# Left queries in 128-wide slices, W1 cast by DMA, and a scheduler for three of five engines

## The chip, the cores and the metric

The kernel runs on one core of a Trainium2 chip. It is timed on the device, in microseconds, from launch to end; lower is better. The engines are TensorE (PE in the profile; PEld its weight loads), VectorE (DVE), ScalarE (ACT), GpSimd (POOL) and SyncE (SP, which here only issues DMAs).

## What is computed

Attention with normalised queries and keys over 8 batches, 12 heads, 448 tokens and 64 elements a head; then a layer normalisation and a two-layer network over the 768 joined elements of each token, added to its input. Inputs and output are FP32.

```
q_n, k_n = rmsnorm(q, g_q), rmsnorm(k, g_k)          # x / sqrt(mean(x*x) + 1e-6) * g
scores = q_n @ k_n.T / 8
attn = exp(scores - max) / (sum + 1e-9)
x = attn @ v                                          # (8, 448, 768)
xn = (x - mean) / sqrt(var + 1e-6) * g_ln
out = x + relu(xn @ w_ch1) @ w_ch2                    # 768 -> 3072 -> 768
```

## The kernel before

**Attention.** Heads go in pairs; a batch has 6 pairs, the kernel 48. q, k and v are loaded by units of 4 heads (two pairs, 24 units), into a tile `t` of 14 groups of 64 elements per partition: 6 groups for each pair's 384 tokens, in three j slices of 128, and one group for its 64 left tokens, of which one head's stand in partitions 0 to 63 and the other's in 64 to 127. `prep_unit` squares q and k on ScalarE, sums on VectorE, takes 1/sqrt by `_rsqrt` (an exponential as first guess, three Newton steps of four operations), multiplies k by g_q*g_k (`gprod`) and by its root, splits it into a high and a low FP16 part side by side (`khl`), and writes q twice side by side (`qn`). v is cast on GpSimd.

`trans_k` and `trans_q` bring each pair's seven 128x128 tiles through TensorE into `ps`, and VectorE copies them to `kT` and `qT`. `scores` makes seven matmuls per pair of 128 keys by 448 queries, the last one (left keys of both heads) in pieces; ScalarE takes the exponential into `E`. `values` multiplies: for each of the seven key tiles, three matmuls with 128 queries as weights (`oA`, L202) and one with the 64 left queries as weights (`oB`, L204). `evac_o` divides by the row sums and writes into the token tiles `x` (three of 128 tokens) and `xl` (left tokens of two batches).

**MLP.** `ln` normalises a batch (three tiles of 128 tokens; a batch of odd number has the left tokens of two batches as a fourth), `ln_trans` transposes into `xnT`. `up` makes `psH` (24 groups of 6 matmuls, 384 or 512 wide) and ScalarE the relu into `hT`; `down` makes `psC` (24 matmuls of 384 for each half tile), VectorE adds x, SyncE stores.

**Weights.** W1 comes in 12 pieces through a staging tile by the SP queue, and GpSimd multiplies each by g_ln into FP16 (`load_w1`, L264). W2 is cast by a DMA from GpSimd's queue (`load_w2`, L268).

**Order.** `run` interleaves: attention is a generator, and after each piece of MLP b it is driven on to the pairs of batch b+1, so that they are through at 0.78 of the MLP's work. The MLP of batch 0 starts after pair 6's scores. The last MLP has no attention beside it. A list scheduler of the kernel's framework then sets the order on all five engines from this text and the dependencies. A second path, `_general`, which a flag chooses where row sums fall outside a range, does not run here.

Of the kernel before, what the change touches and what calls it, by code (L numbers as in the profile page):

```python
# [10 lines left out]
INT32 = mybir.dt.int32  # L11
# [6 lines left out]
LN2 = 0.6931471805599453  # L18
# [5 lines left out]
NU = 3  # L24
UH = H // NU
UG = UH * 3 + UH // 2
EXP_BIAS = -4.0
REC_LO, REC_HI = 1.0 / 3.0e7, 0.5


def _rsqrt(nc, eng, out, a, t0, t1, iters=3):
    eng.tensor_copy(out=t0, in_=a.bitcast(INT32))
    eng.tensor_scalar(out=t0, in0=t0, scalar1=2.0 ** -23, scalar2=-127.0,
                      op0=ALU.mult, op1=ALU.add)
    nc.scalar.activation(out, t0, AFT.Exp, scale=-0.5 * LN2)
    for _ in range(iters):
        eng.tensor_tensor(out=t1, in0=out, in1=out, op=ALU.mult)
        eng.tensor_tensor(out=t1, in0=t1, in1=a, op=ALU.mult)
        eng.tensor_scalar(out=t1, in0=t1, scalar1=-0.5, scalar2=1.5, op0=ALU.mult, op1=ALU.add)
        eng.tensor_tensor(out=out, in0=out, in1=t1, op=ALU.mult)  # L40
# [6 lines left out]
class _Fast:  # L47


    def __init__(self, ctx, tc, sh, q, k, v, w1, w2, out):  # L50
# [5 lines left out]
        self.p_t = pool("p_t", 1)  # L56
# [6 lines left out]
        self.p_st = pool("p_st", 2)  # L63
# [7 lines left out]
        self.v16 = [fix.tile([128, UH, 3, D + 1], FP16, name=f"v{i}", tag=f"v{i}") for i in range(3)]  # L71
        self.vl = [fix.tile([128, UH // 2, 2, D + 1], FP16, name=f"vl{i}", tag=f"vl{i}")
                   for i in range(3)]
        for t in self.kT:
            nc.vector.memset(t[:, 1], 0.0)
        for t in self.v16:
            nc.vector.memset(t[:, :, :, D], 1.0)
        for t in self.vl:
            nc.vector.memset(t, 0.0)
            nc.vector.memset(t[0:64, :, 0, D], 1.0)  # L80
            nc.vector.memset(t[64:128, :, 1, D], 1.0)
        self.rec = fix.tile([128, B * NPAIR, 3, 2], FP32, name="rec_all", tag="rec_all")
# [6 lines left out]
    def load_unit(self, u):  # L89
        nc = self.nc  # L90
        b, hs = u // NU, (u % NU) * UH
        t = self.p_in.tile([128, 3, UG, D], FP32, tag="qkv")
        for n, src in enumerate((self.q, self.k, self.v)):
            nc.sync.dma_start(
                t[:, n, 0:UH * 3].rearrange("p (h j) d -> p h (j d)", j=3),
                src[b, hs:hs + UH, 0:384].rearrange("h (p j) d -> p h (j d)", j=3))
            left = src[b, hs:hs + UH, 384:448].rearrange("(g e) p d -> e p g d", e=2)
            for e in range(2):
                nc.sync.dma_start(t[64 * e:64 * e + 64, n, UH * 3:UG], left[e])
        self.loads[u] = t  # L100

    def prep_unit(self, u):
        nc, sh = self.nc, self.sh
        t = self.loads.pop(u)
        ssq = self.p_n.tile([128, 2, UG], FP32, tag="ssq")
        for n in range(2):
            sq = self.p_t.tile([128, UG, D], FP32, tag="sq", name="sq")
            nc.scalar.activation(sq, t[:, n], AFT.Square)  # L108
            nc.vector.tensor_reduce(out=ssq[:, n], in_=sq, axis=AX.X, op=ALU.add)  # L109
        msq = self.p_n.tile([128, 2, UG], FP32, tag="msq")  # L110
        nc.vector.tensor_scalar(out=msq, in0=ssq, scalar1=1.0 / D, scalar2=1e-6,
                                op0=ALU.mult, op1=ALU.add)
        rr = self.p_n.tile([128, 2, UG], FP32, tag="rr")
        t0 = self.p_n.tile([128, 2, UG], FP32, tag="rt0")
        t1 = self.p_n.tile([128, 2, UG], FP32, tag="rt1")
        _rsqrt(nc, nc.vector, rr, msq, t0, t1)
        qn = self.p_n.tile([128, UG, 2, D], FP16, tag="qn")
        khl = self.p_n.tile([128, UG, 2, D], FP16, tag="khl")
        nc.vector.tensor_tensor(out=t[:, 1], in0=t[:, 1],
                                in1=sh.gprod.unsqueeze(1).broadcast_to([128, UG, D]), op=ALU.mult)  # L120
        nc.vector.tensor_tensor(out=t[:, 1], in0=t[:, 1],
                                in1=rr[:, 1].unsqueeze(2).broadcast_to([128, UG, D]), op=ALU.mult)
        nc.vector.tensor_copy(out=khl[:, :, 0], in_=t[:, 1])
        nc.vector.tensor_tensor(out=khl[:, :, 1], in0=t[:, 1], in1=khl[:, :, 0], op=ALU.subtract)  # L124
        nc.vector.tensor_tensor(out=qn[:, :, 0], in0=t[:, 0],  # L125
                                in1=rr[:, 0].unsqueeze(2).broadcast_to([128, UG, D]), op=ALU.mult)
        nc.vector.tensor_copy(out=qn[:, :, 1], in_=qn[:, :, 0])
        v16, vl = self.v16[u % 3], self.vl[u % 3]
        nc.gpsimd.tensor_copy(out=v16[:, :, :, 0:D],  # L129
                              in_=t[:, 2, 0:UH * 3].rearrange("p (h j) d -> p h j d", j=3))  # L130
        for e in range(2):
            nc.gpsimd.tensor_copy(out=vl[64 * e:64 * e + 64, :, e, 0:D],
                                  in_=t[64 * e:64 * e + 64, 2, UH * 3:UG])
        self.units[u] = (qn, khl, v16, vl)


    def trans_k(self, p):
        nc, sh = self.nc, self.sh
        qn, khl, v16, vl = self.units[p // 2]
        w = p % 2  # L140
        ps = self.ps_tr.tile([128, 1024], FP16, tag="tr")
        kT = self.kT[p % 2]
        gs = [UH * 3 + w] + [6 * w + i for i in range(6)]
        for i, g in enumerate(gs):
            nc.tensor.matmul(ps[:, ts(i, 128)], khl[:, g], sh.id16, is_transpose=True,  # L145
                             start=(i == 0), stop=(i == 6))
        flat = kT.rearrange("p g d -> p (g d)")
        nc.vector.tensor_copy(out=flat[:, 0:64], in_=ps[:, 0:64])  # L148
        nc.vector.tensor_copy(out=flat[:, 128:960], in_=ps[:, 64:896])  # L149

    def trans_q(self, p):
        nc, sh = self.nc, self.sh
        qn, khl, v16, vl = self.units[p // 2]
        w = p % 2
        ps = self.ps_tr.tile([128, 1024], FP16, tag="tr")
        qT = self.p_qT.tile([128, 896], FP16, tag="qT")
        gs = [6 * w, 6 * w + 1, 6 * w + 2, UH * 3 + w, 6 * w + 3, 6 * w + 4, 6 * w + 5]
# [3 lines left out]
        nc.vector.tensor_copy(out=qT, in_=ps[:, 0:896])  # L161
        self.prs[p] = dict(qT=qT, kT=self.kT[p % 2])

    def scores(self, p, i):
# [6 lines left out]
        ps = self.ps_s.tile([128, 512], FP32, tag="psS")  # L171
# [11 lines left out]
    def values(self, p, i):  # L183
        nc = self.nc
        c = self.prs[p]
        qn, khl, v16, vl = self.units[p // 2]
        w = p % 2
        E = c["E"]
        if i == 0:
            c["oA"] = self.ps_o.tile([128, 3, 130], FP32, tag="oA", name="oA")  # L190
            c["oB"] = self.ps_o.tile([64, 130], FP32, tag="oB", name="oB")
        oA, oB = c["oA"], c["oB"]
        if i < 6:
            h, j = divmod(i, 3)
            rhs = v16[:, 2 * w + h, j]
            cs = slice(65 * h, 65 * h + 65)
            m0, l0 = (0, 384) if h == 0 else (64, 0)
        else:
            rhs = vl[:, w].rearrange("p e d -> p (e d)")
            cs, m0, l0 = slice(0, 130), 0, 384  # L200
        for t in range(3):
            nc.tensor.matmul(oA[:, t, cs], E[:, i, m0 + 128 * t:m0 + 128 * t + 128], rhs,  # L202
                             start=(i == 0 and t == 0), stop=(i == 6 and t == 2))
        nc.tensor.matmul(oB[:, cs], E[:, i, l0:l0 + 64], rhs, start=(i == 0), stop=(i == 6))  # L204
# [3 lines left out]
    def evac_o(self, p):  # L208
        nc = self.nc
# [5 lines left out]
        rec, recl = self.rec[:, p], self.recl[:, p]  # L215
        nc.vector.reciprocal(rec, oA[:, :, :, D])
        nc.vector.reciprocal(recl, oB[:, :, D])
        nc.vector.tensor_tensor(  # L218
            out=x[:, :, 128 * hp:128 * hp + 128].rearrange("p t (e d) -> p t e d", e=2),
            in0=oA[:, :, :, 0:D], in1=rec.unsqueeze(3).broadcast_to([128, 3, 2, D]), op=ALU.mult)  # L220
# [3 lines left out]
            in0=oB[:, :, 0:D], in1=recl.unsqueeze(2).broadcast_to([64, 2, D]), op=ALU.mult)  # L224

    def attention(self):

        n = B * NPAIR
        self.load_unit(0)
        self.load_unit(1)  # L230
        self.prep_unit(0)
        self.trans_k(0)
        self.trans_q(0)
        for p in range(n + 1):
# [5 lines left out]
            if p % 2 == 0 and p // 2 + 1 < B * NU:  # L240
                if p // 2 + 2 < B * NU:
                    self.load_unit(p // 2 + 2)
                self.prep_unit(p // 2 + 1)
            for i in range(7):
                if p < n:
                    self.scores(p, i)
                    yield p + (i + 0.5) / 7
                if p > 0:
                    self.values(p - 1, i)
                    yield p + (i + 1) / 7  # L250
                if p + 1 < n and i == 2:
                    self.trans_k(p + 1)
                if p + 1 < n and i == 4:
                    self.trans_q(p + 1)


    def load_w1(self, c0, c1):

        nc, sh = self.nc, self.sh
        st = self.p_st.tile([128, NDC, 256], FP32, tag="st", name="st")  # L260
        nc.sync.dma_start(st[:, :, 0:c1 - c0],
# [354 lines left out]
```

## Time and profile before

| | |
|---|---|
| runs | 796.29, 793.80, 796.85 us; median 796.29 |
| profiled execution | 795.19 us; span from first to last instruction 793.4 us |
| PE | 697.7 us busy (88%), 5114 matmuls |
| DVE | 455.2 us (57%) |
| ACT | 322.0 us (41%) |
| POOL | 119.8 us (15%) |
| mean granted TensorE clock | 0.97 |
| first psH matmul | at 131.4 us |
| start of the last MLP | at 724.2 us |

Busy is the union of an engine's instructions. Rows of groups read: line, engine, operation, out<-in, shape, count, then busy us and mean ns of one, then the idle time ahead of them and what ended it. Rows of the timeline begin with the start and the length in us; a matmul's length is longer than its step, since matmuls follow each other in a pipeline, so steps are read from start to start.

### The profile page before, as it was taken

How to read it: one execution, taken by the hardware profiler on the slowest of the kernel's cores; microseconds unless marked ns; L12 is line 12 of the kernel's file. 1: busy time of each engine (PE TensorE's matmuls, PEld its weight loads, DVE VectorE, ACT ScalarE, POOL GpSimd, SP SyncE). 2: the span in 40 equal slices, each digit the busy share in tenths (PEclk: the TensorE clock that was granted, in tenths of full speed). 3: DMA queues.
4: the chain of work that ended last, by engine and by line, in shares of the span. 5: the costliest groups of instructions: out<-in, count | busy, mean ns of one | idle time of the engine just before them, and what ended most of it. 6: DMA issues, size and time to landing. Idle time of an engine off the chain costs nothing. (4 is left out here: it accounts for less than half of the span.)

```text
span 793.4 us, 12901 instructions
## 1 busy us (share of the span) xinstructions
PE 697.7 (88%) x5114; PEld 419.7 (53%) x5114; DVE 455.2 (57%) x1229; ACT 322.0 (41%) x609; POOL 119.8 (15%) x154
## 2 busy tenths in 40 slices
PE   0276438999999989999999999998999999999996
PEld 0144225655555656656555556655555666664453
DVE  2949369888546783678545683677545452334011
ACT  2163434743364316643464226642464216512400
POOL 2579992000000000010000000010000000000000
PEclk9997777999999999999999999999999999999999
DMA  8993642523021130233022130233020110001011
GB/s 195 239 259 124 190 131 70 140 71 110 21 71 46 61 95 21 70 91 91 21 71 64 47 97 14 70 91 90 21 70 1 40 41 1 2 21 41 0 41 43
DMA packets 76531, 59.17 MB, mean 75 GB/s; under 512 B 23728, under 2 KB 72880, under 8 KB 76464
## 3 DMA queue, kind: packets, MB, share of 16 engines
q1 hardware_dynamic: 72256, 53.49, 22.8%
q0 software_dynamic: 3136, 4.72, 3.3%
q8 instruction: 42, 0.69, 0.4%
q10 hardware_dynamic: 1072, 0.07, 0.1%
q14 instruction: 25, 0.20, 0.1%
HBM read 51.97 MB, written 11.01 MB: 79 GB/s over the span
## 5 line engine op out<-in xcount | busy, mean ns | idle before, releaser
L334 PE MATMUL psC<-w,hT 128*128 128x384 f16 x1344 | 245.8, 329 | 0.0
L323 PE MATMUL psH<-xnT,w 128*128 128x512 f16 (+1 forms) x1152 | 243.3, 353 | 1.8 <-DVE xnT L310 1.8
L180 ACT ACTIVATE E<-ps 128x448 f16<-128x448 f32 x336 | 178.3, 541 | 127.7 <-PE ps L174 100.5
L325 ACT ACTIVATE hT<-psH 128x384 f16<-128x384 f32 (+1 forms) x192 | 104.2, 543 | 162.6 <-PE psH L323 162.6
L334 PEld LDWEIGHTS <-hT 128*128 128x128 f16 x1344 | 125.8, 98 | 77.7 <-issue 1.9
L323 PEld LDWEIGHTS <-w 128*128 128x128 f16 x1152 | 106.5, 98 | 92.2 <-issue 2.6
L174 PE MATMUL ps<-qT,kT 128*128 128x448 f16 x288 | 105.7, 374 | 12.3 <-ACT E L180 7.6
L202 PEld LDWEIGHTS <-E 128*128 128x128 f16 x1008 | 72.7, 100 | 76.2 <-ACT E L180 16.9
L129 POOL CAST v<-t 128x768 f16<-128x768 f32 x24 | 22.0, 917 | 488.8 <-issue 430.5
L202 PE MATMUL oA<-v,E 128*128 128x65 f16 x864 | 74.5, 197 | 16.7 <-ACT E L180 10.4
L109 DVE TENSOR_REDUCE ssq<-sq 128x14 f32<-128x896 f32 x48 | 52.0, 1083 | 64.2 <-ACT sq L108 64.2
L108 ACT ACTIVATE sq<-t 128x896 f32<-128x896 f32 x48 | 45.5, 949 | 80.9 <-DMA t<-in_q_dram 66.0
L264 POOL TENSOR_SCALAR w<-st,gln 128x256 f16<-128x256 f32 x72 | 77.0, 1086 | 9.2 <-DMA st<-in_moe_w_ch_dram 8.9
L338 DVE TENSOR_TENSOR x<-psC,x 128x384 f32<-128x384 f32 x48 | 26.3, 548 | 80.9 <-PE psC L334 80.7
L145 PE MATMUL ps<-id,khl 128*128 128x128 f16 x336 | 29.9, 235 | 38.1 <-DVE khl L124 38.1
L204 PE MATMUL oB<-v,E 128*64 128x65 f16 x288 | 61.5, 219 | 0.4 <-DVE xl L222 0.4
L161 DVE COPY qT<-ps 128x896 f16<-128x896 f16 x48 | 29.7, 619 | 37.7 <-PE ps L159 37.5
L148 DVE COPY kT<-ps 128x64 f16<-128x64 f16 x48 | 9.0, 187 | 69.9 <-PE ps L145 69.7
L204 PEld LDWEIGHTS <-E 128*64 128x64 f16 x336 | 35.3, 107 | 25.3 <-issue 4.3
L145 PEld LDWEIGHTS <-khl 128*128 128x128 f16 x336 | 23.4, 106 | 44.7 <-DVE khl L124 38.4
L174 PEld LDWEIGHTS <-kT 128*128 128x128 f16 x288 | 27.9, 99 | 17.0 <-issue 5.3
L159 PE MATMUL ps<-id,qn 128*128 128x128 f16 x336 | 28.6, 228 | 5.1 <-DVE kT L149 4.9
(71 smaller groups left out, 549.7 us busy)
## 6 DMA issues: line engine op xcount, KB each, us to landing
t<-in_q_dram SPq DMA_DIRECT2D x24, 384.0 KB, 3.5
t<-in_k_dram SPq DMA_DIRECT2D x24, 384.0 KB, 4.3
t<-in_v_dram SPq DMA_DIRECT2D x24, 384.0 KB, 4.4
st<-in_moe_w_ch_dram SPq DMA_DIRECT2D x12, 768.0 KB, 5.1
out_dram<-x SPq DMA_DIRECT2D x24, 384.0 KB, 2.3
w<-in_moe_w_ch_dram POOLq DMA_DIRECT2D x4, 1152.0 KB, 13.4
t<-in_q_dram SPq DMA_DIRECT2D x48, 32.0 KB, 3.7
t<-in_k_dram SPq DMA_DIRECT2D x48, 32.0 KB, 3.8
```

Of the source, the lines that this page charges most:

```text
L108: nc.scalar.activation(sq, t[:, n], AFT.Square)
L109: nc.vector.tensor_reduce(out=ssq[:, n], in_=sq, axis=AX.X, op=ALU.add)
L145: nc.tensor.matmul(ps[:, ts(i, 128)], khl[:, g], sh.id16, is_transpose=True, start=(i == 0), stop=(i == 6))
L161: nc.vector.tensor_copy(out=qT, in_=ps[:, 0:896])
L174: nc.tensor.matmul(ps[:, 0:S], kT[:, 192 + 128 * i:320 + 128 * i], qT[:, h * S:(h + 1) * S], start=True, stop=True)
L180: nc.scalar.activation(out=c["E"][:, i], in_=ps[:, 0:S], func=AFT.Exp, scale=1.0 / 8.0, bias=EXP_BIAS)
L202: nc.tensor.matmul(oA[:, t, cs], E[:, i, m0 + 128 * t:m0 + 128 * t + 128], rhs, start=(i == 0 and t == 0), stop=(i == 6 and t == 2))
L204: nc.tensor.matmul(oB[:, cs], E[:, i, l0:l0 + 64], rhs, start=(i == 0), stop=(i == 6))
L264: nc.gpsimd.tensor_scalar(out=sh.w1[:, dc, c0:c1], in0=st[:, dc, 0:c1 - c0], scalar1=sh.gln[:, dc:dc + 1], scalar2=None, op0=ALU.mult)
L323: nc.tensor.matmul(ps[:, 0:N], sh.w1[:, dc, ts(f, 128)], xnT[:, dc, 0:N], start=(dc == 0), stop=(dc == NDC - 1))
L325: nc.scalar.activation(out=hT[:, f, 0:N], in_=ps[:, 0:N], func=AFT.Relu)
L334: nc.tensor.matmul(ps[:, 0:384], hT[:, f, ts(t, 128)], sh.w2[:, f, ts(g, 384)], start=(f == 0), stop=(f == NFF - 1))
```

## The change

1. `oB` now takes queries 320 to 447 as weights (128 columns) and has 128 rows, of which the last 64 are used; both heads keep their left queries last, so `qT` is copied in three parts, and the seventh score tile has two matmuls of 448 where it had 448, 384 and 64.
2. W1 is cast by three DMAs from GpSimd's queue; g_ln is applied to the normalised tokens instead, on VectorE, after ScalarE has normalised (`norm`). W2 comes in two DMAs for four.
3. Batch 0 is loaded in six units of one pair, into parts of `hT`; the other units have two pairs. The left tokens of units 0 and 1 are loaded by the ACT queue, ahead of its first work. k is loaded first.
4. The product with `gprod` moves to GpSimd. The squares are written into the buffers of `khl` and `qn`. `_rsqrt` has two Newton steps of three operations, and a unit's preparation is dealt out over the pairs before it (`prep_ops`).
5. Layer statistics are taken pair by pair in pieces of 128 elements (`stats`); `ln_ops` deals out the rest. Step 0 of the values moves one chunk later. Attention is through at 0.82 of the MLP.
6. GpSimd and SyncE keep the text's order; the list scheduler orders the other three engines.

The core of the diff:

```diff
-def _rsqrt(nc, eng, out, a, t0, t1, iters=3):
-    eng.tensor_copy(out=t0, in_=a.bitcast(INT32))
-    eng.tensor_scalar(out=t0, in0=t0, scalar1=2.0 ** -23, scalar2=-127.0,
-                      op0=ALU.mult, op1=ALU.add)
-    nc.scalar.activation(out, t0, AFT.Exp, scale=-0.5 * LN2)
-    for _ in range(iters):
-        eng.tensor_tensor(out=t1, in0=out, in1=out, op=ALU.mult)
-        eng.tensor_tensor(out=t1, in0=t1, in1=a, op=ALU.mult)
-        eng.tensor_scalar(out=t1, in0=t1, scalar1=-0.5, scalar2=1.5, op0=ALU.mult, op1=ALU.add)
-        eng.tensor_tensor(out=out, in0=out, in1=t1, op=ALU.mult)
+def _rsqrt(nc, out, a, t, eps):
+    eng = nc.vector
+    eng.tensor_scalar(out=a, in0=a, scalar1=eps, scalar2=None, op0=ALU.add)
+    nc.scalar.activation(out, a.bitcast(INT32), AFT.Exp, scale=-0.5 * LN2 * 2.0 ** -23,
+                         bias=0.5 * LN2 * (127.0 - 0.043))
+    for _ in range(2):
+        eng.tensor_tensor(out=t, in0=out, in1=out, op=ALU.mult)
+        eng.scalar_tensor_tensor(out=t, in0=t, scalar=-0.5, in1=a, op0=ALU.mult, op1=ALU.mult)
+        eng.scalar_tensor_tensor(out=out, in0=t, scalar=1.5, in1=out, op0=ALU.add, op1=ALU.mult)
...
+        eng = nc.scalar if u < 2 else nc.sync
+        for n, src in ((1, self.k), (0, self.q), (2, self.v)):
             nc.sync.dma_start(
...
+                eng.dma_start(t[64 * e:64 * e + 64, n, mh * 3:g], left[e])
...
+        def square(n):
+            o = c["khl" if n == 1 else "qn"].rearrange("p g e d -> p (g e d)").bitcast(FP32)
+            c["sq", n] = o.rearrange("p (g d) -> p g d", d=D)
+            nc.scalar.activation(c["sq", n], c["t"][:, n], AFT.Square)
...
+        def kg():
+            nc.gpsimd.tensor_tensor(out=c["t"][:, 1], in0=c["t"][:, 1],
+                                    in1=sh.gprod.unsqueeze(1).broadcast_to([128, g, D]),
+                                    op=ALU.mult)
...
-        nc.vector.tensor_copy(out=qT, in_=ps[:, 0:896])
+        nc.vector.tensor_copy(out=qT[:, 0:448], in_=ps[:, 0:448])
+        nc.vector.tensor_copy(out=qT[:, 448:832], in_=ps[:, 512:896])
+        nc.vector.tensor_copy(out=qT[:, 832:896], in_=ps[:, 448:512])
...
-            nc.tensor.matmul(ps[:, 0:384], kT[:, 64:192], qT[:, 512:896], start=False, stop=False)
-            nc.tensor.matmul(ps[:, 384:448], kT[:, 64:192], qT[:, 448:512], start=False, stop=True)
+            nc.tensor.matmul(ps[:, 0:S], kT[:, 64:192], qT[:, S:2 * S], start=False, stop=True)
...
-        nc.tensor.matmul(oB[:, cs], E[:, i, l0:l0 + 64], rhs, start=(i == 0), stop=(i == 6))
+        nc.tensor.matmul(oB[:, cs], E[:, i, 320:448], rhs, start=(i == 0), stop=(i == 6))
...
-                    self.values(p - 1, i)
-                    yield p + (i + 1) / 7
+                    for x in {0: (), 1: (0, 1)}.get(i, (i,)):
+                        self.values(p - 1, x)
...
-        st = self.p_st.tile([128, NDC, 256], FP32, tag="st", name="st")
-        nc.sync.dma_start(st[:, :, 0:c1 - c0],
-                          self.w1[:, c0:c1].rearrange("(dc p) f -> p dc f", p=128))
-        for dc in range(NDC):
-            nc.gpsimd.tensor_scalar(out=sh.w1[:, dc, c0:c1], in0=st[:, dc, 0:c1 - c0],
-                                    scalar1=sh.gln[:, dc:dc + 1], scalar2=None, op0=ALU.mult)
+        self.nc.gpsimd.dma_start(
+            out=self.sh.w1[:, :, c0:c1],
+            in_=self.w1[:, c0:c1].rearrange("(dc p) f -> p dc f", p=128))
...
+            nc.scalar.activation(out=t32, in_=tiles[t], func=AFT.Identity,
+                                 scale=c["rs"][:, t:t + 1], bias=c["sh"][:, t:t + 1])
+            nc.vector.tensor_tensor(out=c["xn", t], in0=t32, in1=sh.gln, op=ALU.mult)
...
-        frac = 0.78
+        frac = 0.82
...
-        _Fast(fctx, tc, sh, q, k, v, moe_w_ch1, moe_w_ch2, out).run()
+        with tc.manual_schedule(engines={ENG.Pool, ENG.SP}):
+            _Fast(fctx, tc, sh, q, k, v, moe_g_ln, moe_w_ch1, moe_w_ch2, out).run()
```

Three places in the order show what moves. The first is GpSimd's queue in the start, before; `w_73` is W1, `w_74` W2, `v` and `vl` the FP16 values, `st` the staging tile:

```order
L268 DMA w_74<-in_moe_w_ch_dram 128x6x768
L264 TENSOR_SCALAR w_73<-st,gln 128x256 x12
L268 DMA w_74<-in_moe_w_ch_dram 128x6x768
L129 CAST v_121<-t 128x12x64
L132 CAST vl_124<-t 64x2x64 x2
L264 TENSOR_SCALAR w_73<-st,gln 128x256 x6
L129 CAST v_119<-t 128x12x64
L132 CAST vl_122<-t 64x2x64 x2
L264 TENSOR_SCALAR w_73<-st,gln 128x256 x30
L129 CAST v_120<-t 128x12x64
```

The same stretch after, where `hT` and `t` hold loaded units, `w_72` is W1 and `w_73` W2:

```order
L145 TENSOR_TENSOR hT<-hT,gprod 128x448
L315 DMA w_72<-in_moe_w_ch_dram 128x6x1024 x3
L166 CAST v_114<-hT 128x6x64
L171 CAST vl<-hT 64x64 x2
L145 TENSOR_TENSOR hT<-hT,gprod 128x448
L166 CAST v_114<-hT 128x6x64
L171 CAST vl<-hT 64x64 x2
L145 TENSOR_TENSOR hT<-hT,gprod 128x448
L166 CAST v_114<-hT 128x6x64
L320 DMA w_73<-in_moe_w_ch_dram 128x12x768 x2
```

The multiplications are gone; W1's DMAs stand behind the product with `gprod` of unit 2, W2's behind that of unit 4, and each unit's product stands ahead of its v cast.

The second is TensorE's queue within MLP work, a key tile's values and what follows them, before:

```order
L202 MATMUL oA<-v_119,E 128x65
L202 LDWEIGHTS E
L202 MATMUL oA<-v_119,E 128x65
L204 LDWEIGHTS E
L204 MATMUL oB<-v_119,E 64x65
L159 LDWEIGHTS qn
L159 MATMUL ps<-id_58,qn 128x128
```

and after:

```order
L241 MATMUL oA<-v_114,E 128x65
L241 LDWEIGHTS E
L241 MATMUL oA<-v_114,E 128x65
L243 LDWEIGHTS E
L243 MATMUL oB<-v_114,E 128x65
L200 LDWEIGHTS qn
L200 MATMUL psQ<-id_58,qn 128x128
```

The number of value matmuls stays, and what follows them; oB's outputs go from 64 to 128 rows.

The third is the SP queue around the stores of an MLP of odd number, before:

```order
L353 DMA out_dram<-x 128x768 x2
L94 DMA t<-in_q_dram 128x4x192
L99 DMA t<-in_q_dram 64x2x64 x2
L94 DMA t<-in_k_dram 128x4x192
L99 DMA t<-in_k_dram 64x2x64 x2
L94 DMA t<-in_v_dram 128x4x192
L99 DMA t<-in_v_dram 64x2x64 x2
L353 DMA out_dram<-x 128x768
L356 DMA out_dram<-xl 64x768 x2
L94 DMA t<-in_q_dram 128x4x192
```

and after:

```order
L106 DMA t<-in_v_dram 128x4x192
L111 DMA t<-in_v_dram 64x2x64 x2
L424 DMA out_dram<-x 128x768 x3
L427 DMA out_dram<-xl 64x768 x2
L106 DMA t<-in_k_dram 128x4x192
L111 DMA t<-in_k_dram 64x2x64 x2
L106 DMA t<-in_q_dram 128x4x192
L111 DMA t<-in_q_dram 64x2x64 x2
```

The five stores now stand together ahead of the loads; before, a whole unit's loads stood between them.

More of the change, by code (lines that the diff above doesn't have):

```diff
@@ L98, in load_unit, with prep_ops @@
             for e in range(2):
-                nc.sync.dma_start(t[64 * e:64 * e + 64, n, UH * 3:UG], left[e])
+                eng.dma_start(t[64 * e:64 * e + 64, n, mh * 3:g], left[e])
         self.loads[u] = t
-    def prep_unit(self, u):
+    def prep_ops(self, u):
         nc, sh = self.nc, self.sh
[L104 to L134, printed above, removed]
```

325 lines of the change are left out of this document (191 added, 134 removed).

## The prediction

> **What bounds the kernel now.** I read the page's slices first, then the span cut into three stages, then the step from one matmul to the next in the timeline. Durations come from the profiled execution (795.19 us, span 793.4); it stands 1.1 us under the median of the runs, so nothing is corrected for that.
>
> The stages are cut where the first psH matmul begins and where the last MLP begins:
>
> ```profile
> core 0: us, PE busy (x) PEld busy (x) DVE busy (x) ACT busy (x) POOL busy (x), PEclk, DMA share, GB/s
> 0.00:131.40 131.40, 58.84 (x492) 37.41 (x493) 85.25 (x234) 46.56 (x85) 92.62 (x103) 0.86 0.71 182
> 131.40:724.20 592.80, 576.52 (x4289) 349.61 (x4289) 364.90 (x987) 261.10 (x500) 27.21 (x51) 0.99 0.19 56
> 724.20:793.40 69.20, 62.29 (x337) 32.67 (x334) 5.02 (x9) 14.33 (x24) 0.00 (x0) 0.97 0.09 30
> ```
>
> Stage 1 (attention of batch 0, no MLP yet) leaves TensorE idle more than half the time; GpSimd is the busiest engine. Stage 2 is TensorE from end to end (97%), and so is stage 3, whose last 6.9 us are evacuation and store. So two things are worth asking: when does the first psH start, and how much issue time does TensorE need from there.
>
> GpSimd is what paces stage 1. In its timeline 30 of the 72 W1 multiplications stand in one piece, and the v casts of two units stand behind such pieces:
>
> ```profile
> 60.58 33.05 POOL L264 TENSOR_SCALAR w<-st,gln 128x256 f16<-128x256 f32 x30 [1.12 <-DMA st<-in_moe_w_ch_dram]
> 93.59 0.82 POOL L129 CAST v<-t 128x768 f16<-128x768 f32 x1
> 95.09 25.08 POOL L264 TENSOR_SCALAR w<-st,gln 128x256 f16<-128x256 f32 x24
> ...
> 131.38 2.94 PE L323 MATMUL psH<-xnT,w 128*128 128x384 f16 x17
> ```
>
> The first psH comes 11 us after the last of them ends (120.2). Where VectorE is not held it is nearly full: 18.99 of 20 us here, against 85.25 of 131.4 over the stage.
>
> ```profile
> 60.00:80.00 20.00, 12.39 (x106) 7.79 (x105) 18.99 (x51) 6.71 (x13) 19.42 (x17) 0.74 0.35 116
> ```
>
> For stage 2, the steps (start to next start, us in the first column):
>
> ```profile
> 300.14 0.25 PE L202 MATMUL oA<-v,E 128*128 128x65 f16 x3
> 300.32 0.22 PE L204 MATMUL oB<-v,E 128*64 128x65 f16 x1
> 300.48 0.56 PE L145 MATMUL ps<-id,khl 128*128 128x128 f16 x7
> 300.88 0.35 PE L174 MATMUL ps<-qT,kT 128*128 128x448 f16 x1
> 301.07 1.14 PE L323 MATMUL psH<-xnT,w 128*128 128x384 f16 x6
> 302.04 0.25 PE L202 MATMUL oA<-v,E 128*128 128x65 f16 x3
> ...
> 588.23 1.47 PE L323 MATMUL psH<-xnT,w 128*128 128x512 f16 x6
> 589.54 0.35 PE L174 MATMUL ps<-qT,kT 128*128 128x448 f16 x1
> ...
> 644.44 1.14 PE L334 MATMUL psC<-w,hT 128*128 128x384 f16 x6
> 645.41 0.50 PE L308 MATMUL psX<-id,xn 128*128 128x128 f16 x6
> ...
> 101.20 0.71 PE L202 MATMUL oA<-v,E 128*128 128x65 f16 x18 [0.64 <-DVE t L37]
> 101.75 0.54 PE L174 MATMUL ps<-qT,kT 128*128 128x448 f16 x2
> ```
>
> A transpose takes 0.056 (7 in 0.40), a score 0.19, a psH 0.162 (6 in 0.97, 384 wide) or 0.218 (6 in 1.31, 512 wide), a psC 0.162. The reader is to see the value matmuls: 18 oA in a row, each with 128 weight columns, take 0.55, or 0.031 each. But three oA and one oB take 0.34 (300.14 to 300.48), where four at 0.031 would be 0.12. The oB (128*64, 64 weight columns) costs 0.21 too much: the load neither runs beside the matmul ahead of it nor lets the next load start.
>
> **The sum for stage 2.** Before: 532 transposes of k and q x 0.056 = 29.8; 150 of xn = 8.4; 39 pairs of scores x (6 x 0.19 + 0.38) = 59.3; 1092 value matmuls, 936 x 0.031 and 156 of 130 wide at the 0.056 of a 128-wide one = 37.7; 273 oB x 0.21 = 57.3; psH 576 x 0.162 + 432 x 0.218 = 187.5; psC 1152 x 0.162 = 186.6. Together 566.6 of 592.8, so 26 are lost, half of it in these waits and the rest in small slips:
>
> ```profile
> PE psX L308 <- DVE xn L298: 6.5, 4, 2.0
> PE oA L202 <- DVE x L218: 5.3, 10, 1.8
> PE psH L323 <- DVE xnT L310: 1.8, 2, 0.9
> ```
>
> After: oB runs E[320:448], 128 weight columns, so its 0.21 goes; the counts are otherwise the same but for one pair's values and a k transpose group (+1.3). That gives 511. The two score matmuls of 384 and 64 become one of 448: nothing.
>
> The Trainium skill, page "TensorE: Matmul & The Clock Gate", section "LDWEIGHTS (loading the stationary operand)", speaks against this step: a load takes its columns divided by 1.2 in ns, so 64 columns cost 53 and 128 cost 107, and 273 loads would lose 15 us instead of gaining 57 (785 in all, an estimate from that page). Its section "Weight-path perf modes — Fast Weight Load (FWL) and DoubleRow" has the other half: loads of exactly 128 columns, not FP32, take a faster path. The trace decides for the second: 0.031 a step leaves no room for 107 ns.
>
> What else lies on TensorE's path in stage 2: the value matmuls of step 0 move one chunk later, behind the evacuation of the pair before, which takes most of the 5.3 of "oA <- x"; the statistics are taken pair by pair, which shortens the chain ahead of psX; ScalarE then has the normalisation, and VectorE the product with g_ln. Against that all chunks come faster by 0.2, so every transpose copy has less time. I take the loss as 30 (bounds 15, the named waits gone by half, and 60, twice as much as now).
>
> **VectorE, ScalarE, GpSimd in stage 2.** Their work must fit into 541 us instead of 593:
>
> ```profile
> L119 DVE TENSOR_TENSOR t<-t,gprod 128x896 f32<-128x896 f32 x6 | 6.5, 1081 | 0.0
> L161 DVE COPY qT<-ps 128x896 f16<-128x896 f16 x10 | 6.2, 617 | 5.9 <-PE ps L159 5.7
> L39 DVE TENSOR_SCALAR t<-t 128x28 f32<-128x28 f32 x16 | 4.4, 275 | 0.3
> L40 DVE TENSOR_TENSOR rr<-rr,t 128x28 f32<-128x28 f32 x15 | 4.3, 284 | 0.2
> L292 DVE BATCH_NORM_STATS2 stat<-x 128x6 f32<-128x384 f32 x6 | 3.3, 546 | 0.0
> L148 DVE COPY kT<-ps 128x64 f16<-128x64 f16 x10 | 1.9, 186 | 4.4 <-PE ps L145 4.3
> ...
> L39 DVE TENSOR_SCALAR t<-t 128x28 f32<-128x28 f32 x72 | 14.3, 199 | 1.9
> L108 ACT ACTIVATE sq<-t 128x896 f32<-128x896 f32 x48 | 45.5, 949 | 80.9 <-DMA t<-in_q_dram 66.0 <-DVE ssq L109 6.2 <-DMA t<-in_k_dram 6.1
> L264 POOL TENSOR_SCALAR w<-st,gln 128x256 f16<-128x256 f32 x72 | 77.0, 1086 | 9.2 <-DMA st<-in_moe_w_ch_dram 8.9
> L129 POOL CAST v<-t 128x768 f16<-128x768 f32 x24 | 22.0, 917 | 488.8 <-issue 430.5 <-PE oB L204 32.9 <-DMA t<-in_v_dram 20.3
> ```
>
> VectorE per unit of two pairs: the g product goes (-1.08), the root has 7 small operations for 15 (-1.6 at 0.2); per pair qT comes in three copies (0.39 + 0.35 + 0.19 on the line through L161 and L148, +0.31), statistics in pieces of 128 at half of L292 (+0.3). Net -1.5 a unit: about 340 of 541, 63% as now. ScalarE gains 25 normalisations of 0.83 (L108 scaled to 768), 21 us: 282 of 541, 52%; hidden, 21 if it were not. GpSimd gains the g product, which no row shows: below, the cast L129 gives 1.1 for 896 elements, above, the multiplication L264 gives 3.8; I take 2.4, between, since it has one input more than the cast. 19 of them are 46 us on an engine that stood idle 95% of stage 2. None is the bound on average.
>
> **Stage 1.** The 72 multiplications (77.0 us) and the 12 W1 loads on the SP queue go. W1 comes in three casting DMAs on GpSimd's queue, behind the g product of unit 2, which waits for unit 2's k and its square; that square needs unit 0's khl buffer, so unit 0's transposes. With the first square at 15 (below) and an estimated 9 us for unit 0's chain, they are issued near 24. The nearest rows:
>
> ```profile
> w<-in_moe_w_ch_dram POOLq DMA_DIRECT2D x4, 1152.0 KB, 13.4
> t<-in_q_dram SPq DMA_DIRECT2D x24, 384.0 KB, 3.5
> ...
> 9.36 1.28 ACT L108 ACT_TABLE_LOAD   x1 [9.36 <-DMA t<-in_q_dram]
> ...
> SPq L353 <- DVE x L338: 196.3, 12, 53.3
> ```
>
> W1 writes 4.7 MB, four times the 1152 KB of 13.4 us: 55 us one after the other, in by 79. W2's two DMAs go out behind unit 4's product and are needed 24 psH groups after the first, some 30 us with the scores between them. Both are covered, W1 by 23 us; without that cover the first psH waits for W1.
>
> ScalarE now issues 12 small loads of units 0 and 1 ahead of its table load. Each waits for a semaphore of an earlier one, eight in all, so about three waves of 3.5 to 4.4 and 1.28 for the table: first square near 15, against 10.65. Then VectorE paces: 85.25 of busy time now; minus 6.5 (L119), minus 8.4 (19 of root operations, 8 units x 7 x 0.19 in their place), plus 2.8 (qT), plus 2.7 (six small units for three large: fixed parts), plus 2.1 (statistics), minus 3.6 (a pair's copies and evacuation and one sum fewer in the stage): 74. At 85% busy, nearer to the 95% of the free slice than to the 65% of the stage, it takes 87. First psH at 102; bounds 89 (always busy) and 129 (65%).
>
> **Total**: 102 + 511 + 30 + 69.2 (stage 3, unchanged) + 1.8 (around the span) = 714, of which the start brings 29 and the oB loads 57.
>
> **Rivals.**
> The start stays as long: VectorE at 65%, or W1 late because nothing but GpSimd's queue carries it. First psH at 129: 741. For it: ScalarE's squares must wait for transposes two units back, and the queues of GpSimd and SP are in program order. Against: GpSimd's 33 us piece is gone.
>
> The slips in stage 2 double to 60: 744. VectorE's load is 63% on average but more where attention runs (82% of each MLP), and GpSimd's product collides with it: L39 takes 275 in stage 1, beside the W1 multiplications, and 199 over the whole run. It decides if each of 40 pairs slips by 0.75. The Trainium skill ("SBUF — State Buffer", section "Who interferes with whom") says why: a VectorE operation with two SBUF inputs and a reading GpSimd operation exclude each other for a whole instruction; by that each product could hold VectorE for 2.4.
>
> The wide load does not help, the 0.21 belonging to oB's place and not its width: 714 + 57 = 771. Against: oA has the same operands and rows.
>
> Slower: SP in program order holds loads behind the stores of an MLP (L353 waited up to 53.3 us in that queue), and the next units' transposes stand still. Loads go out two units, some 25 us, ahead of use; if a store is later than that by 12 us at each of 7 batch ends, 84 us are lost, 798, and beyond that it is slower. Against: stores stand in the order in which TensorE makes the sums.
>
> **How the numbers follow.** Forecast 0.70 (685 to 735), long start 0.11, slips 0.08, no help from width 0.05, slower 0.04, better than 685 0.02. The range 685 to 752 leaves out the last three and joint cases. The bound of no change is 0.5%: faster 0.95, same 0.01, slower 0.04.
>
> **What would show it.** Right: oB steps of 0.03, first psH near 102 with no GpSimd piece over 4 us, TensorE over 94% busy between it and the last MLP. Wrong: oB still followed by 0.15; psH waiting for w; transposes of k or q waiting for VectorE more than 10 us in sum; the SP queue waiting for a store while TensorE is idle.

## The result, and the profile after

The changed kernel takes 739.8 us (median of 741.59, 738.06, 746.12 and 736.90) against 795.0 for the kernel before on the same chip: ratio 0.932 (95% interval 0.925 to 0.940). On a second chip it took 740.1 against 797.2, ratio 0.929 (0.924 to 0.934). The profiled execution took 741.59, its span 739.8.

The windows by stage of the changed kernel, with the columns as before (length; PE, PEld, DVE, ACT and POOL busy; granted clock, DMA share, GB/s):

```profile
0.00:123.20 123.20, 54.95 (x448) 32.55 (x449) 82.77 (x236) 48.80 (x96) 33.31 (x48) 0.76 0.74 159
123.20:670.00 546.80, 522.69 (x4282) 323.05 (x4281) 346.66 (x950) 278.49 (x526) 62.19 (x72) 0.98 0.21 61
670.00:739.80 69.80, 62.72 (x339) 32.77 (x337) 5.34 (x11) 14.33 (x24) 0.00 (x0) 0.97 0.09 30
```

Stage 2 fell from 592.8 to 546.8, where 541 was forecast. Stage 1 fell from 131.4 to 123.2, where 102 was forecast. Of the 26 us by which the forecast was too low, 21 lie in stage 1 and 6 in stage 2 (the profiled execution is 2 us longer than the median), so two questions follow: why is VectorE only 67% busy there (82.77 of 123.2), and is stage 2 right for the right reasons?

The timeline of TensorE shows the value matmuls of the changed kernel:

```profile
181.89 0.26 PE L241 MATMUL oA<-v,E 128*128 128x65 f16 x3
181.98 0.19 PE L243 MATMUL oB<-v,E 128*128 128x65 f16 x1
182.01 0.26 PE L241 MATMUL oA<-v,E 128*128 128x65 f16 x3
182.10 0.20 PE L243 MATMUL oB<-v,E 128*128 128x65 f16 x1
182.14 0.25 PE L241 MATMUL oA<-v,E 128*128 128x65 f16 x3
```

Three oA and one oB take 0.12 from start to start (181.89 to 182.01), where they took 0.34: the 0.21 of each oB is gone. What TensorE waits for in stage 2 (us in total, times, longest) is new on its second row:

```profile
PE psX L379 <- DVE xn L366: 11.7, 9, 2.5
PE psQ L200 <- DVE kT L190: 11.3, 11, 1.6
```

In stage 1 the groups of ScalarE from 36 to 81 us give the place (busy, mean ns, then idle time ahead and what ended it):

```profile
L136 ACT ACTIVATE khl<-hT 128x448 f32<-128x448 f32 x2 | 1.2, 576 | 8.4 <-DMA hT<-in_k_dram 8.4
L136 ACT ACTIVATE qn<-hT 128x448 f32<-128x448 f32 x2 | 1.2, 576 | 8.2 <-DMA hT<-in_q_dram 8.2
L136 ACT ACTIVATE khl<-t 128x896 f32<-128x896 f32 x1 | 0.9, 949 | 8.5 <-DMA t<-in_k_dram 8.5
L136 ACT ACTIVATE qn<-t 128x896 f32<-128x896 f32 x1 | 0.9, 949 | 5.8 <-DMA t<-in_q_dram 5.8
```

For 31 of these 45 us ScalarE stands at six squares whose k or q has not landed, with the exponentials behind them (the tile names `hT` and `t` are loaded units, `khl` and `qn` the places of the squares). The window of the same stretch and the DMA issues up to 130 us (size, median us from issue to landing) say why:

```profile
36.00:81.00 45.00, 18.72 (x148) 11.08 (x147) 25.33 (x79) 12.87 (x28) 8.52 (x12) 0.62 1.14 220
```

```profile
w<-in_moe_w_ch_dram POOLq DMA_DIRECT2D x3, 1536.0 KB, 21.3
w<-in_moe_w_ch_dram POOLq DMA_DIRECT2D x2, 2304.0 KB, 29.7
t<-in_k_dram SPq DMA_DIRECT2D x4, 384.0 KB, 9.2
t<-in_q_dram SPq DMA_DIRECT2D x4, 384.0 KB, 7.3
```

The DMA share is 1.14, so the DMA engines are counted busy all the time. W1 (issued at 26.7) and W2 (at 49.7) run beside the loads of units 3 to 7. The 384 KB loads of k and q take 9.2 and 7.3 us, where they took 4.3 and 3.5 in the profile before (all medians); VectorE, behind the squares, is 25.33 of 45 busy. The granted clock of 0.62 does not explain it: TensorE is busy only 18.72 of the 45 us, and what ends ScalarE's waits are the loads. The Trainium skill ("DMA: Bandwidth & Descriptors", section "Queues, rings and completion order") says that each DMA engine goes round the queues it has work for, packet by packet; the landing times agree with that: a later small load lands in 7 to 9 us while the long ones take 21 to 30, so it shares with them and does not stand behind them.

### The profile page after: what moved, and what is told of

Same layout as the page of the kernel before. It is cut to its first block, busy times and chain, and to the rows that moved or that the text cites. A ratio compares the mean times of both kernels' runs of the same rounds, so it can differ in the third digit from the quotient of the medians.

```text
span 739.8 us, 12904 instructions
## 1 busy us (share of the span) xinstructions
PE 640.4 (87%) x5066; PEld 388.4 (52%) x5066; DVE 434.8 (59%) x1195; ACT 341.6 (46%) x646; POOL 95.5 (13%) x119
## 4 chain that ended last, share of the span: by engine, by line
PE 56%; DVE 20%; ACT 3%; issue 2%; DVEq 0%; ACTq 0%
PE psH L394 26%; PE psC L405 17%; PE psS L217 4%; PE oA L241 2%; DVE ssq L139 2%; DVE qn L47 2%; PE psQ L200 2%; DVE stat L339 2%; ACT qn L136 2%; PE psX L379 1%; DVE t L47 1%; DVE khl L156 1%; PE psK L186 1%; DVE x L258 1%; DVE xn L366 1%
## 5 line engine op out<-in xcount | busy, mean ns | idle before, releaser
L222 ACT ACTIVATE E<-psS 128x448 f16<-128x448 f32 x336 | 177.6, 540 | 95.4 <-PE psS L217 81.8
L217 PE MATMUL psS<-qT,kT 128*128 128x448 f16 x288 | 105.0, 376 | 31.2 <-ACT E L222 19.4
L145 POOL TENSOR_TENSOR t<-t,gprod 128x896 f32<-128x896 f32 x21 | 44.7, 2127 | 383.4 <-issue 151.9
L241 PEld LDWEIGHTS <-E 128*128 128x128 f16 x1008 | 70.2, 102 | 43.0 <-issue 3.2
L186 PE MATMUL psK<-id,khl 128*128 128x128 f16 x336 | 30.3, 232 | 28.7 <-DVE rt L40 23.9
L243 PE MATMUL oB<-v,E 128*128 128x65 f16 x288 | 49.5, 199 | 2.2 <-DVE xl L263 2.2
L200 PE MATMUL psQ<-id,qn 128*128 128x128 f16 x336 | 29.0, 231 | 15.7 <-DVE kT L190 15.7
L139 DVE TENSOR_REDUCE ssq<-khl 128x14 f32<-128x896 f32 (+1 forms) x27 | 26.4, 979 | 20.2 <-ACT khl L136 20.2
L243 PEld LDWEIGHTS <-E 128*128 128x128 f16 x336 | 32.2, 100 | 7.7 <-issue 5.4
L339 DVE BATCH_NORM_STATS2 stat<-x 128x6 f32<-128x128 f32 x144 | 34.0, 283 | 1.3
L258 DVE TENSOR_TENSOR x<-oA,rec_all 128x384 f32<-128x384 f32 x48 | 26.8, 558 | 9.9 <-DMA out_dram<-x 8.5
```

The lines of the kernel that those rows point to most:

```text
L139: nc.vector.tensor_reduce(out=c["ssq"][:, n], in_=c["sq", n], axis=AX.X, op=ALU.add)
L145: nc.gpsimd.tensor_tensor(out=c["t"][:, 1], in0=c["t"][:, 1], in1=sh.gprod.unsqueeze(1).broadcast_to([128, g, D]), op=ALU.mult)
L200: nc.tensor.matmul(ps[:, ts(i, 128)], qn[:, g], sh.id16, is_transpose=True, start=(i == 0), stop=(i == 6))
L217: nc.tensor.matmul(ps[:, 0:S], kT[:, 192 + 128 * i:320 + 128 * i], qT[:, h * S:(h + 1) * S], start=True, stop=True)
L222: nc.scalar.activation(out=c["E"][:, i], in_=ps[:, 0:S], func=AFT.Exp, scale=1.0 / 8.0, bias=EXP_BIAS)
L241: nc.tensor.matmul(oA[:, t, cs], E[:, i, ts(t, 128)], rhs, start=(i == 0 and t == 0), stop=(i == 6 and t == 2))
```

## The experiments

All on the changed kernel. "First psH" and "stage 2" are read from each run's profile; ratios are to the kernel before on the same chip.

| run | first psH | stage 2 | time | ratio |
|---|---|---|---|---|
| changed kernel, first and second chip | 123.2, 124.9 | 546.8, 542.4 | 739.8, 740.1 | 0.932, 0.929 |
| a1, weights not loaded | 102.9 | (549.6) | 724.0, one run | |
| a2, W2 two pairs later | 116.3 | 549.7 | 736.0 | 0.920 (0.916 to 0.925) |
| a3, eight units loaded first | 111.2 | 545.6 | 727.2 | 0.909 (0.906 to 0.913) |
| b1, the same, W2 later in the text | 110.7 | 545.5 | 727.8 | 0.913 (0.909 to 0.917) |
| c1, the same, W2 behind unit 8's v cast | 102.1 | 550.2 | 719.0 | 0.898 (0.894 to 0.901) |
| b3, g product on VectorE | 125.9 | 540.6 | 740.6 | 0.929 (0.925 to 0.934) |
| c3, list scheduler on all engines | 122.4 | 542.7 | 738.6 | 0.924 (0.920 to 0.927) |
| a4, oB with 64 columns | 125.4 | 581.3 | 778.9 | 0.976 (0.972 to 0.980) |
| b2, large kT copy on ScalarE | 122.4 | 553.3 | 748.2 | 0.937 (0.934 to 0.941) |
| c2, pacing 0.78 | 124.3 | 529.1 | 725.9 | 0.908 (0.904 to 0.911) |
| c4, c1 and c2 together | 101.4 | 529.5 | 702.8 | 0.878 (0.876 to 0.881) |

**Is it the weights?** In a1 they are not loaded, so the output is that of other weights and only stage 1 is read; in a2 only W2 is moved:

```diff
 a1:
-        for c in range(0, FF, 1024):
-            self.load_w1(c, c + 1024)
-        upto(3)
-        for n0 in range(0, NFF, 12):
-            self.load_w2(n0, n0 + 12)
+    nc.vector.memset(sh.w1, 0.01); nc.gpsimd.memset(sh.w2, 0.01)     # ahead of all units
 a2:
-        upto(3)
+        upto(5)
         for n0 in range(0, NFF, 12):
```

> W1 and W2 are not loaded at all (both are filled with a constant before the first unit, on engines that stand idle there), so the output is that of other weights; only stage 1 is read from this run. Contention theory: the two weights fill the DMA engines from 27 to 90 us (share 1.14 in 36 to 81) and the q and k loads of units 3 to 7 come late behind them; ScalarE stands at their squares (31 us of waits for q and k loads between 36 and 81) and everything behind it. Without the weights these waits fall below 5 us and the first psH comes at 95 to 103 instead of 123. Rival, order: the loads are late because their slots come free late and SyncE goes in program order; then ScalarE still waits over 20 us and the first psH stays at 115 or later. Rival, VectorE: the 83 us of VectorE work at 75 to 80% busy set the pace; first psH 105 to 112.

> W2's two DMAs are issued after five pairs of attention instead of three (near 80 us instead of 50). Contention theory: W1 is in by 70 and the loads of units 6 and 7 meet no weight; the two waits of 8.5 and 5.8 us near 64 to 80 go for the most part, the first psH comes at 108 to 115 and the whole time is 725 to 733. W2 would be in near 115 and is needed near 140. Order rival: no change, 737 to 745.

The first psH of a1 comes at 102.9, as the contention theory had it (95 to 103) and 20 us earlier than in the changed kernel. The same stretch in a1:

```profile
36.00:81.00 45.00, 30.53 (x254) 17.50 (x252) 44.20 (x129) 27.20 (x53) 12.70 (x20) 0.73 0.38 101
```

DMA share 0.38 for 1.14, and VectorE 44.2 of 45 us busy for 25.3. The loads of k and q land in half the time:

```profile
t<-in_k_dram SPq DMA_DIRECT2D x4, 384.0 KB, 3.6
t<-in_q_dram SPq DMA_DIRECT2D x4, 384.0 KB, 4.1
```

With the weights out of the way VectorE sets the pace of stage 1, with the loads' slots and order unchanged, so the order rival falls. (The two fills take 15 us each, ahead of the first square, which comes at 17.1 for 16.1.) a2 moves the first psH to 116.3, a little past its 108 to 115, and takes 736.0, past its 725 to 733: half the traffic moved away, a third of the loss gone.

**Can it be had with the weights?** a3 loads the six units of batch 0 into the place of W2, which comes after their last use, and the first two of batch 1 right behind; b1 differs only in the position of W2 in the text.

```diff
-            o = 2688 * (u % 3)
-            t = self.hT.rearrange("p f n -> p (f n)")[:, o:o + 2688].bitcast(FP32)
+            o = 2688 * u
+            t = self.sh.w2.rearrange("p f n -> p (f n)")[:, o:o + 2688].bitcast(FP32)
...
-            if u + 2 < nu and u + 2 > 2:
+            if u + 2 < nu and u + 2 > 7:
...
-        for u in range(3):
+        for u in range(8):
             self.load_unit(u)
...
-        upto(3)                       # ahead of load_w2
+        upto(5.5)                     # a3; 6.9 in b1; in c1 load_w2 stands behind ln_ops(0)
```

> All six units of batch 0 and the first two of batch 1 are loaded ahead of everything else, the six into the place where W2 comes later (so that no slot has to come free first), and W2 is issued after five and a half pairs. Contention theory and order rival agree that ScalarE's waits for q and k fall below 8 us; then the first psH comes at 98 to 107 and the time is 715 to 725. VectorE rival: VectorE is over 85% busy from 36 on and the first psH is at 108 or later, 725 or more. If W2 came too late for the first psC (needed near 130 us), the loss would show as a wait of psC for w.

> The eight first units loaded ahead of everything, as before, and W2 issued after 6.9 pairs instead of 5.5. There W2 was issued at 67.7 us, while W1 was still coming, and units 7 and 8 were late (5.9 and 8.2 us of ScalarE's waits). Contention theory: with W2 behind them these go, VectorE stays over 90% busy to the end of stage 1, the first psH comes at 99 to 105 and the time is 715 to 721. Against it: W2's first half, issued near 85, would have to be in by 135; if its transfer takes over 40 us, psC waits for w and the gain goes. Rival (VectorE paces anyway): 108 to 111, 724 to 728.

> The eight first units loaded ahead of everything; W2 issued behind the v cast of unit 8 on GpSimd's queue (in the text after the normalisation of batch 0), since the position in the text alone did not delay it: GpSimd had no work to wait for ahead of it and issued it at 68 us in both versions before. Contention theory: units 7 and 8 now meet no weight, ScalarE's waits for q and k after 36 us fall below 4 us, W2 goes out at 88 to 96 and its first half is in by 120 (first psC needed near 133); first psH at 99 to 104, 715 to 721. If something else holds stage 1 (VectorE beside GpSimd, transposes two units back), the first psH stays at 108 to 111 and the time at 724 to 728.

a3 gains 12 us in stage 1 and misses its range by 4. Its numbers (111.2 and 727.2) are those of the VectorE rival, but not its cause, since VectorE is far from full in the last 30 us of the stage:

```profile
81.00:111.20 30.20, 14.80 (x151) 8.74 (x150) 18.66 (x57) 14.53 (x27) 3.91 (x5) 0.77 0.83 174
```

b1, which was to gain the rest, changes nothing. The timelines of GpSimd and then of ScalarE in b1 show the error in that edit:

```profile
67.80 0.82 POOL L166 CAST v<-t 128x768 f16<-128x768 f32 x1
68.56 2.08 POOL L320 DMA_DIRECT2D w<-in_moe_w_ch_dram  x2
70.63 1.47 POOL L171 CAST vl<-t 64x128 f16<-64x128 f32 x2
88.19 2.07 POOL L145 TENSOR_TENSOR t<-t,gprod 128x896 f32<-128x896 f32 x1 [16.09 <-ACT khl L136]
```

```profile
87.11 0.95 ACT L136 ACTIVATE khl<-t 128x896 f32<-128x896 f32 x1 [5.66 <-DMA t<-in_k_dram]
94.86 0.95 ACT L136 ACTIVATE qn<-t 128x896 f32<-128x896 f32 x1 [5.94 <-DMA t<-in_q_dram]
```

W2 went out at 68.6 for 67.7 in a3: in an engine's program order a place in the text delays nothing unless an instruction ahead of it waits. Unit 8's loads (75 to 87 us) met W2 and ScalarE stood at its squares. In c1 W2 stands behind unit 8's product and v cast, where GpSimd waits 13 us; it is issued at 86.8, and VectorE is nearly full to the end of the stage:

```profile
81.00:102.00 21.00, 14.87 (x153) 9.01 (x151) 20.04 (x58) 14.01 (x26) 6.52 (x6) 0.86 0.79 151
```

The first psH comes at 102.1, in the expected range, with the same bytes loaded: it was when they were loaded.

**The other suspects for stage 1.** b3 sets `nc.vector` for `nc.gpsimd` in `kg`; c3 drops `tc.manual_schedule(...)`.

> The product of k with gprod goes back to VectorE (0.6 us for a unit of one pair, 1.08 for two). Theory, contention by loads in stage 1: VectorE has slack there (67% busy), and what its operations lose beside GpSimd's product (0.17 becoming 1.07) comes back, so the first psH stays within 3 us of 123; in stage 2 it adds 21 us of work to an engine that is busy 63% and late at the batch ends, stage 2 longer by 0 to 6; 738 to 749. Rival, port: the exclusion between GpSimd's product and VectorE is what makes stage 1 long; then the first psH comes at 113 or earlier and the time is 726 to 733.

> The list scheduler orders all five engines, so GpSimd and SyncE leave the program order. Theory: program order on these two matters only where weights and loads meet; the scheduler can issue the loads of q, k and v and the weights' DMAs earlier or later, so the first psH moves by up to 10 us either way (113 to 130) and stage 2 by less than 5: 730 to 750. Rival, program order is what keeps loads ahead of stores: stores of an MLP and loads change places on SyncE, and ScalarE waits for q and k in stage 2 too, 750 or more.

Neither changes the time by more than its interval. In b3 VectorE has some 7 us more work in stage 1 (6 x 0.6 + 3 x 1.08) and yet is busy 81.6 us against 82.0 in the changed kernel on the same chip: what the product takes on GpSimd it costs VectorE in operations that take longer beside it (the twelve `rt<-rr` of 128x14 take 412 ns each in the changed kernel and 174 in b3). In c3 the first W1 DMA goes out at 1.3 us, and ScalarE has its first load only at 23.3, for 14.8 in the changed kernel: what the weights gain there, the first loads pay.

**Was the oB term right?** a4 sets oB back to 64 weight columns:

```diff
-            c["oB"] = self.ps_o.tile([128, 130], FP32, tag="oB", name="oB")
+            c["oB"] = self.ps_o.tile([64, 130], FP32, tag="oB", name="oB")
...
-        nc.tensor.matmul(oB[:, cs], E[:, i, 320:448], rhs, start=(i == 0), stop=(i == 6))
+        nc.tensor.matmul(oB[:, cs], E[:, i, 384:448], rhs, start=(i == 0), stop=(i == 6))
```

> oB is set back to 64 weight columns and 64 rows, all else stays as changed. Width theory: each of the 273 oB of stage 2 costs 0.21 us more, +57 us; those in stage 1 lie beside other waits; 792 to 802 (ratio to the kernel before about 1.00). Rival, place: the 0.21 belonged to the place of oB in the row and not to its width, no change: 737 to 747. In between (765 to 780) the load's 0.21 would be partly hidden where stage 2 waits for VectorE.

The timeline of TensorE in a4, and its waits in stage 2:

```profile
188.79 0.26 PE L241 MATMUL oA<-v,E 128*128 128x65 f16 x3
188.97 0.22 PE L243 MATMUL oB<-v,E 128*64 128x65 f16 x1
189.12 0.27 PE L241 MATMUL oA<-v,E 128*128 128x65 f16 x3
```

```profile
PE psX L379 <- DVE xn L366: 5.7, 9, 1.9
PE psH L394 <- DVE xnT L381: 0.6, 1, 0.6
PE psQ L200 <- DVE kT L190: 0.5, 2, 0.3
```

The step is back at 0.33, so the width is the cause and the size of 0.21 holds. But stage 2 grew by 35 to 39 (against 546.8 and 542.4), not by 57. The time, 778.9, is the in-between case of the expectation. The rest is in the waits: psQ and psX wait 6.2 us here and 23.0 in the changed kernel. It nearly closes: all waits of stage 2 are 6.8 us here and 24.5 on the second chip, the lost clock (below) 0 and 3.4; 57.3 less 17.7 less 3.4 is 36.2, and 38.9 was measured (on the first chip 31.2 and 34.5). So 18 to 23 of the 57 us of the wide load come back, nearly all as new waits and lost clock: a pair is now through 1.5 us sooner (7 x 0.21), and the waits are for VectorE.

**Where, and whose queue?** The end of batch 2's MLP in the changed kernel, TensorE's timeline and windows over the wait:

```profile
343.64 0.19 PE L243 MATMUL oB<-v,E 128*128 128x65 f16 x1
343.67 0.28 PE L241 MATMUL oA<-vl,E 128*128 128x130 f16 x2
345.55 0.56 PE L200 MATMUL psQ<-id,qn 128*128 128x128 f16 x7 [1.60 <-DVE kT L190]
...
347.41 0.82 PE L379 MATMUL psX<-id,xn 128*128 128x128 f16 x6 [1.19 <-DVE xn L366]
...
349.41 0.85 PE L405 MATMUL psC<-w,hT 128*128 128x384 f16 x2
```

```profile
345.00:347.00 2.00, 0.68 (x9) 0.51 (x9) 2.00 (x3) 1.98 (x3) 0.00 (x0) 0.95 0.00 0
347.00:349.00 2.00, 1.59 (x11) 1.15 (x12) 1.95 (x4) 2.00 (x4) 0.00 (x0) 0.50 0.00 0
```

VectorE is full (2.00 of 2.00), TensorE waits for it, and no psC stands in between. After the wait the granted clock is 0.50 for a while. Added up over windows of 1 us, such spells in stage 2 cost 8.5 us of clock in this profile, 3.4 in the one on the second chip, 11.9 in c1's and none in c2's; that is most of the spread of stage 2 among runs with the same program there (542 to 550). b2 takes work from VectorE's queue, c2 gives the batch ends more MLP work:

```diff
 b2:
-        nc.vector.tensor_copy(out=flat[:, 128:960], in_=ps[:, 64:896])
+        nc.scalar.activation(flat[:, 128:960], ps[:, 64:896], AFT.Identity)
 c2:
-        frac = 0.82
+        frac = 0.78
```

> The large copy of the k transposes (832 elements, 0.58 us, once a pair) moves from VectorE to ScalarE; the scheduler reorders some steps on TensorE. In stage 2 TensorE waits 11.3 us with psQ for that copy, since both transposes use one PSUM tile and the copy stands in VectorE's queue behind other work. Theory, VectorE's queue: psQ waits under 5 us in stage 2, stage 2 at 540 to 543; stage 1 shorter by 2 to 4, since VectorE has 4 us less there; 730 to 736. Rival, ScalarE's queue: the copy stands behind exponentials of 0.54 each and psQ waits as long or longer, psS waits for E; 739 to 750.

> Only the pacing is set back: attention of the next batch is through at 0.78 of an MLP's work, as in the kernel before, and not at 0.82. Theory, batch ends: psQ and psX wait (20 to 23 us in stage 2) where the last pairs of a batch have run out of MLP work beside them; with 0.78 more psC stand there, the two waits fall to 10 to 16 us in sum and stage 2 takes 534 to 541 (542 to 547 with 0.82); 729 to 737. Rival, VectorE is too full while attention runs: denser attention makes the waits for kT and qT longer everywhere; stage 2 548 or more, 744 or more.

b2 is 8 us slower than the changed kernel on the same chip, as its ScalarE rival had it, though the intervals just touch. Its waits in stage 2:

```profile
PE psX L379 <- DVE xn L366: 17.0, 8, 3.3
PE psQ L200 <- ACT kT L190: 10.7, 9, 1.8
```

The wait for kT is nearly the same from another engine, so it is not VectorE's queue alone that makes it. Of the 10.9 us by which stage 2 is longer than on the same chip, 4.8 are these two waits and 6.8 lost clock (10.2 for 3.4). Why psX waits longer is not shown: VectorE's operation ahead of it, xn, waits for ScalarE 3.9 us in both.

c2 takes 725.9 us, less than expected. Its timeline shows 42 psC behind the last oB of batch 3, in the MLP of batch 2, where the changed kernel (second row) has 30; the waits of stage 2 follow:

```profile
331.88 0.22 PE L243 MATMUL oB<-vl,E 128*128 128x130 f16 x1
331.93 6.99 PE L405 MATMUL psC<-w,hT 128*128 128x384 f16 x42
```

```profile
336.00 5.04 PE L405 MATMUL psC<-w,hT 128*128 128x384 f16 x30
```

```profile
PE psX L379 <- DVE xn L366: 12.3, 7, 1.8
PE oA L241 <- DVE x L258: 1.3, 2, 0.7
PE psQ L200 <- DVE kT L190: 1.3, 1, 1.3
```

psQ's 11.3 is down to 1.3 and psX's is as it was; in sum they are 13.6, in the expected 10 to 16. The transposes psQ that waited 1.60 at 345.55 in the changed kernel, ahead of psX, come at 353.58 in c2, between psH of the next MLP, and wait for nothing. All waits together fell by 8.5, the lost clock by 8.5: 17.0 of the 17.7 by which stage 2 is shorter than on the first chip (13.3 against the second). The theory of the batch ends holds for psQ, not for psX, and half of the gain against the first chip is clock that c2 did not lose.

**Both.**

> Both together: the eight first units ahead of everything with W2 behind unit 8's v cast, and the pacing at 0.78. If the two losses are separate (one in stage 1, one at the batch ends), they add up: first psH at 100 to 104, stage 2 at 527 to 533, in all 700 to 709. If stage 2 without the late start of W2 and with more psC at the batch ends only moves the wait elsewhere (loads of batch 1 beside W2, first psC waiting for w), stage 2 takes 540 or more, 712 or more.

```profile
0.00:101.40 101.40, 50.31 (x447) 29.74 (x448) 80.07 (x236) 47.98 (x95) 29.59 (x47) 0.87 0.73 160
101.40:630.90 529.50, 515.09 (x4284) 319.30 (x4284) 344.64 (x951) 277.05 (x527) 63.49 (x72) 1.00 0.25 69
630.90:700.50 69.60, 62.43 (x338) 32.75 (x336) 5.00 (x10) 14.33 (x24) 0.00 (x0) 0.97 0.09 30
```

The windows by stage of c4: the two losses were separate and add up. It takes 702.8 us, ratio 0.878 where the changed kernel has 0.929 to 0.932, and its six runs lie between 702.4 and 704.0, where the changed kernel's spread over 8 to 9 us.

> The changed kernel itself, once more, on the chip of the three experiments beside it, so that small steps can be read against it: 737 to 745, first psH at 122 to 125.

This was the changed kernel beside b1 to b3, as in the table.

## The prediction, point by point

- The time, 739.8, lies above the forecast of 685 to 735 and inside the wider range only through the rivals.
- **oB: right.** Steps of 0.03, and undoing it shows 0.21 each. Of the two rules of the Trainium skill ("TensorE: Matmul & The Clock Gate") that were weighed, the columns divided by 1.2 (section "LDWEIGHTS (loading the stationary operand)") would have made it slower by 15; the run decides for the fast path of 128 columns (section "Weight-path perf modes — Fast Weight Load (FWL) and DoubleRow").
- **Loss of stage 2, 30: 36, by another way than told.** Work of 511 and a stage of 546.8. The "oA <- x" wait went, as said; but the sign set down as wrong came (transposes waiting over 10 us in sum: psQ 11.3). With the narrow load and the same pacing the loss is 13 (581.3 less 511 and 57.3), with 0.78 it is 18. Of the 36 here, 24 are waits and 8.5 lost clock, which the sum did not have. The term was nearly right by luck: a gain (with the narrow load 13 for the 26 of the kernel before; which part of the change made it was not taken apart) and a loss (0.82 with faster chunks) met in it. 0.82 was listed as part of the change and given no price; it costs 13 to 18 us, 3.4 and 8.5 of them lost clock.
- **First psH, 102: 123.2, the step that failed.** Small parts held: first square 16.1 (15), W1 issued at 26.7 (24), GpSimd's product 2.13 us for 896 elements (2.4). VectorE's work was 82.8 and not 74: what it loses beside GpSimd's product, 7 us, was named only as a rival for stage 2 (b3 has 81.6 with 7 of product in it, so the sum of the rest holds). But the 21 us come from the sentence "Both are covered": it asked only whether the weights arrive in time, not what their transfers (28 to 87 us) do to the loads that share the DMA engines. On arrival it was even too careful: the slowest of W1's DMAs landed 29.6 us after its issue, where the sum had 55 for W1. The profile before gave a warning: from 20 to 40 us its DMA share is 1.10, with the loads of W1, W2 and the units side by side. Without the weights, and with them in another order (c1), the stage takes 102.9 and 102.1. That this is the forecast 102 is partly luck: c1's VectorE has 78 us of work from 16 us on and is 91% busy, where the sum had 74 at 85%.
- **The long start as rival: right in its time (741) and its 65% of VectorE (67%), wrong in its reasons.** W1 was not late, dropping the program order on GpSimd and SyncE changes nothing measurable (c3, where weights gain and first loads lose), and in a1 the squares wait 8.6 us for transposes (psK and psQ) without effect, since VectorE is full.
- **The slower rival did not come:** in stage 2 the squares wait 0.2 us in all for q or k, though SyncE holds stores for up to 44 us.
- **VectorE 340, ScalarE 282, stage 3 69.2:** 346.7, 278.5 and 69.8.

## What to carry to other kernels

Price a prefetch twice: whether it arrives in time, and which transfers land late while it runs; where the DMA share is full, first issue what is needed first, and make the long one wait on an instruction that really waits, since a place in the text is no delay on an engine in program order. When a step on the busiest engine becomes shorter, set the pacing of the work beside it anew: here 18 to 23 of 57 us were lost again, mostly in waits for the copies between and in clock, and a pacing number brought 13 to 18 back.

## What the runs showed of the hardware

- TensorE waits of 1 to 2.5 us can bring a second loss: the granted clock stood at 0.50 for 3.4 or 6.8 us behind some of them, which made 3 to 12 us per execution where the program of stage 2 was the changed kernel's. Which waits set it off is not settled: after the one of 1.55 us at 186 nothing followed, and the two at 344 to 347, which set it off in the profile on the first chip, did not in that on the second, where they are as long. The Trainium skill ("TensorE: Matmul & The Clock Gate", "Part 1: The HAM clock gate (the "warmup" mystery)") tells of half the clock after an idle window of about 3.4 us, which agrees with the length of the single spells (3.41); but no single wait of stage 2 was that long (the longest 2.5 in the changed kernel).
- Moving a 1.08 us product from VectorE to GpSimd saved VectorE nothing in stage 1 (81.6 busy with it, 82.0 without) and 14 of 19 us in stage 2 (360.1 and 346.3).
